# Attended values in a PSUM bank of their own, an MLP ring of three banks, and a re-planned instruction list

## The chip, the cores and the metric

The kernel runs on one core of a Trainium2 chip, as one launch. The metric is the device time of that launch in microseconds (us). Three runs of the kernel before gave 1077.95, 1076.28 and 1081.45 us, so the median is 1077.95 us. One execution was also recorded by the hardware profiler: it took 1077.04 us, and its trace covers a span of 1075.3 us of that.

The core has five engines that work beside each other, each on its own queue in order: PE (matrix products, written to PSUM), DVE (vector engine), ACT (scalar engine), POOL (GpSimd) and SP, which here only starts transfers. An engine waits at an instruction until the semaphores that it names have been raised. PSUM, the memory that PE writes, has eight banks per partition, each of 512 float32; DVE and ACT read it.

## The reference, cut to what matters

```python
# q, k, v: (4, 8, 576, 64); attention with the 32 largest scores of each row
scores = q @ k.T / sqrt(64)
kth    = 32nd largest of each row
attn   = softmax(where(scores >= kth, scores, -1e9))
x      = (attn @ v), heads side by side       # (2304, 512)
# first MLP, 512 -> 2048 -> 512
h = x @ w_in
g = where(h > 0, h, exp(min(h, 0)) - 1)
x = g @ w_out
# second MLP, 512 -> 1024 -> 512
h   = ((x @ w1) * (x @ w2)) @ w3
out = h @ w_out2
```

All inputs are float32 in the reference; the weights reach the kernel as 64-bit words, of which it makes float32 values on the chip, and of these a float16 pair (high and low part) for three float16 products per float32 product.

## The kernel before, in words

**Tiles.** The 2304 tokens are 18 tiles of 128. Nine chunks of two tiles each run through attention and then through the MLP. For a chunk, attention goes over four pairs of heads and the two tiles: 72 steps in all (and eight of them straddle two batches, so that they have two segments).

**One attention step.** SP loads a tile of q (`qr`), ACT and POOL split it (L414, L415). For each of the two heads PE forms 128 x 576 scores as two halves of 288 columns, one in each of the two banks of the PSUM tile `psS` (L435, four matmuls, called QK below), and ACT copies them to `s` (L437, the score copy). DVE finds the 32 largest with four MAX8 (L445) and three MATCH_REPLACE8 (L447). ACT turns the scores to weights (L460, L462), ACT and POOL split them to float16 pairs `pi` (L470, L471), a transposing DMA brings them to `pt` (L473). PE multiplies them by the values (L489, 28 matmuls for a segment, called AV below) into an accumulator `psA`; column 64 of each head is the sum of the weights. ACT copies the sums (L500), DVE inverts them (L503) and multiplies (L506, to `xf`), ACT and POOL split the result (L509, L510), and a small transposing DMA puts it into the MLP's input `x` (L511).

**PSUM before.** `psS` has two banks, `psY` two, and the ring `psR` four, so all eight are taken. The two accumulators `psA` are columns 288 to 417 of the two banks of `psS`, behind the score columns, and are used in turn.

**MLP.** A unit A is 24 matmuls of 256 columns (L748 to L750) into one bank of `psR`; ACT reads it twice (L760 and L769). A unit O (L785 to L787) adds to `psY`. A unit B is 24 matmuls (L827 to L829) into one bank of `psR`, read by ACT (L837, or L846) and DVE (L847). A unit D (L862 to L864) uses a bank of `psR` too. `rot()` hands out the banks of the ring in the order in which the program is written.

**Weights.** Before and beside the first chunks, 72 blocks of weights are loaded and made float32 (`load64`): ACT writes a helper value into a bank of the ring (L540), DVE reads it (L541), ACT and POOL finish (L542, L543). `norm` (L335, L337, L340, L341) measures the size of a set of blocks by way of one or two banks.

**What sets the order.** Nothing runs in the order in which it is written. `Program.op` gathers every operation with its engine, an estimated cost, what it reads and writes, and a due time, to which the table `OFF` adds a number for its group (for example `A2:PE`). `emit` plays the list through a model of the engines and takes, whenever an engine is free, the ready operation with the lowest rank; the model's order is what each engine then gets. For a transfer the model has a time at which it lands (L179). The model orders by the keys that an operation names: in the kernel before `psA` has a key of its own, apart from that of `psS`.

Of the kernel before, what the change touches and what calls it, by code (L numbers as in the profile page):

```python
# [8 lines left out]
F32 = mybir.dt.float32  # L9
# [30 lines left out]
OFF = {":DVE": 12998, "A0:ACT": 1029, "A0:PE": 7709, "A0:POOL": 27517, "A1:ACT": 718, "A1:PE": -1966, "A1:POOL": -5070, "A2:ACT": 9368, "A2:PE":  # L40
# [25 lines left out]
       -37249, "att8x:SP": 2491, "attsa:ACT": -34761, "attsa:PE": -24674, "attsk:ACT": -25447, "attsk:POOL": -12314, "attsk:SP": 6109, "attsm:ACT":  # L66
       58721, "attsm:POOL": 42862, "attsp:ACT": -13632, "attsp:POOL": 6842, "attsp:SP": 1004, "attsq:ACT": -6686, "attsq:POOL": 29332, "attsq:SP":
       2937, "attss:ACT": -4807, "attss:PE": 439, "attst:DVE": 42919, "attsv:ACT": 36078, "attsv:DVE": 24193, "attsv:SP": 27657, "attsx:ACT": 19116,
# [3 lines left out]
       "w_in.c:PE": 6093, "w_in.n:DVE": -7844, "w_in.n:PE": 4153, "w_in:ACT": 4398, "w_in:DVE": -6625, "w_in:POOL": -6043, "w_in:SP": -40971,  # L72
       "w_out.c:ACT": -366, "w_out.c:DVE": -7456, "w_out.c:PE": -21835, "w_out.n:DVE": -33383, "w_out.n:PE": -12498, "w_out:ACT": -1295, "w_out:DVE":
       11860, "w_out:POOL": 17259, "w_out:SP": 13558, "w_v0:DVE": -35479, "w_v0:PE": 32785, "w_v0:SP": -8488, "w_v1:DVE": -18213, "w_v1:PE": 29747,
       "w_v1:SP": 53184, "w_v:DVE": -41841}
# [18 lines left out]
class Program:  # L94
# [30 lines left out]
    def emit(self):  # L125
# [22 lines left out]
        for _ in range(n):  # L148
# [23 lines left out]
            if e == "SP":  # L172

                if len(done) >= 8:
                    t = max(t, done[-8])
                begin = max(dma, t + (1100.0 if lat < 500.0 else 1275.0))
                free[e] = max(t + lat, begin + 131.0) if lat > 1300.0 else t + lat
                dma = begin + cost
                end = dma + 900.0  # L179
                done.append(end)  # L180
            else:
                end = free[e] = t + cost
# [13 lines left out]
def kernel(ctx: ExitStack, tc: tile.TileContext, qd, kd, vd, vn, w_in, w_out, w1, w2, w3t, w4, out,  # L196
# [56 lines left out]
    psAs = [psS[:, i, 288:418].rearrange("p (h d) -> p h d", h=2) for i in range(2)]  # L253
    psY = ring("psY", 2, [128, 2, 256], F32, psum)
    psR = ring("psR", 4, [128, 512], F32, psum)
    psN, pnk = psY[0].rearrange("p a b -> p (a b)")[:, 0:128], ("psY", 0)
    banks = [0, 1]
# [136 lines left out]
    def attention(c, t0, n):  # L394
# [6 lines left out]
        for pair in range(4):  # L401
            base = (t0 * 8 + pair * n * 2 + PAR["a0"] * (c == 0) + PAR["a1"] * (c == 1)) * STEP
            for t in range(n):
# [76 lines left out]
                pa = nxt("psA", 2)  # L480
                psA, pak = psAs[pa], ("psA", pa)
                for bb, c0, c1 in segs:
                    vs = Vc[bb, pair]

                    def av(vs=vs, c0=c0, c1=c1, pt=pt, psA=psA):
                        for hh in range(2):
                            for j in range(14):
                                d = 65 if j < 9 else 64
                                T.matmul(psA[c0:c1, hh, 0:d], lhsT=PT[pt][:, hh, j % 9, c0:c1], rhs=VV[vs][:, j, hh, 0:d], start=j == 0, stop=j == 13, skip_group_check=True)  # L489
                    op("PE", 930, av, [("v", vs), ("vl", vs), ("pt", pt, 0), ("pt", pt, 1)], [pak], p5)  # L490
# [6 lines left out]
                for c0, c1 in ((0, r1), (r1, 128)):  # L497
                    if c0 < c1:
                        sc_, sk_ = (scal(f"rho{vb}")[c0:c1], [("rho", vb)]) if c0 < r1 else (1.0, [])
                        op("ACT", 190, lambda psA=psA, dn=dn, c0=c0, c1=c1, sc_=sc_: A.activation(dn[c0:c1], psA[c0:c1, :, 64], AF.Copy, scale=sc_, bias=1e-9), [pak, *sk_], [K("dn")], p5)  # L500
# [4 lines left out]
                def xfin(xf=xf, dn=dn, psA=psA):  # L505
# [17 lines left out]
    def load64(dst, key, src, shape, pr, slots_, nm, whole=False):  # L523
# [14 lines left out]
        lb = 2 if nm == "w12" else 2 + nxt("low", 2)  # L538
# [48 lines left out]
    def prep_v(b, pr):  # L587
# [12 lines left out]
        norm(pieces, nv, kb, pr)  # L600
# [319 lines left out]
    for c, n in enumerate(chunks):  # L920

        s1 = starts[c] + n
        for b in range(batch(s1) + 1 if c else 1, batch(s1 + (chunks[c + 1] if c + 1 < len(chunks) else 0)) + 1):
            keep, banks[:] = banks[:], [3] if len(banks) < 4 else banks
            prep_v(b, (s1 * 8 + PAR["pvb"]) * STEP)
            banks[:] = keep
        attention(c, starts[c], n)
        if c >= 1:
# [3 lines left out]
            banks[:] = [0, 1] if c == 1 else [0, 1, 2, 3]  # L932
# [58 lines left out]
```

## Time and profile before

| | |
|---|---|
| median of three runs | 1077.95 us |
| profiled execution | 1077.04 us |
| span of its trace | 1075.3 us |
| PE busy | 983.4 us, 91% of the span |
| DVE busy | 889.3 us, 83% |
| ACT busy | 830.3 us, 77% |
| POOL busy | 696.6 us, 65% |
| transfers | 174.97 MB, mean 163 GB/s |

Busy time is that of the instructions of an engine's datapath; waiting at a semaphore is idle time. A wait is named by the line that waited and the line that released it. Matmuls overlap in their pipeline, so PE counts as busy where one is still draining: the step from one matmul to the next is shorter than the time of one. PEclk is the clock that PE was granted as a share of the full one.

### The profile page before, as it was taken

What the parts mean: (1) busy time and instruction counts of PE and PEld (TensorE: products, weight loads), DVE (VectorE), ACT (ScalarE), POOL (GpSimd) and SP (SyncE); (2) the same over time, 40 slices, a digit from 0 to 9 for tenths busy, and PEclk for the clock granted to TensorE, in tenths of its full rate; (3) what the DMA queues carried; (4) which work ended last, traced back from release to release, by engine and by line L of the source; (5) the groups of instructions that cost most, each with busy time, mean ns of one, the idle gap of its engine ahead of it and who ended that gap; (6) DMA issues with size and microseconds to landing.
All of it is one profiled execution on the core that took longest, in us unless ns stands there. A gap on an engine that the chain in (4) does not pass through costs nothing. (4 is left out here: it accounts for less than half of the span.)

```text
span 1075.3 us, 24646 instructions
## 1 busy us (share of the span) xinstructions
PE 983.4 (91%) x9132; PEld 778.6 (72%) x9132; DVE 889.3 (83%) x1968; ACT 830.3 (77%) x1521; POOL 696.6 (65%) x743
## 2 busy tenths in 40 slices
PE   4486899988899989989999999999999999999998
PEld 2333455677787778868887887788778877887875
DVE  4999999999999889998968999998899999810010
ACT  6999887898989867878887797798778878824512
POOL 4967565699478645776884597488547846645611
PEclk9998999989899999999999999999999999999999
DMA  9979997498675794577877738686855373032001
GB/s 362 391 224 297 288 257 173 146 269 178 157 176 164 190 201 116 106 184 182 202 195 180 161 47 198 175 197 156 183 147 118 95 160 69 2 63 63 1 1 40
DMA packets 255384, 174.97 MB, mean 163 GB/s; under 512 B 196640, under 2 KB 223264, under 8 KB 255264
## 3 DMA queue, kind: packets, MB, share of 16 engines
q1 hardware_dynamic: 255264, 173.41, 63.3%
q8 instruction: 71, 1.16, 0.5%
q14 instruction: 49, 0.40, 0.1%
HBM read 104.56 MB, written 21.61 MB: 117 GB/s over the span
## 5 line engine op out<-in xcount | busy, mean ns | idle before, releaser
L445 DVE MAX8 m<-wk 128x8 f32<-128x576 f32 x432 | 311.3, 747 | 0.8
L471 POOL TENSOR_TENSOR pi<-s,pi 128x576 f16<-128x576 f32 x144 | 185.2, 1294 | 92.3 <-ACT pi L470 72.1
L447 DVE MATCH_REPLACE8 wk<-m,wk 128x576 f32<-128x576 f32 x288 | 212.4, 742 | 0.0
L786 PE MATMUL psY<-g,wout 128*128 128x256 f16 x576 | 157.6, 274 | 1.5 <-POOL g L772 1.5
L748 PE MATMUL psR<-x,win 128*128 128x256 f16 x576 | 157.2, 273 | 1.5 <-ACT t L837 0.8
L827 PE MATMUL psR<-x,w 128*128 128x256 f16 x576 | 158.4, 275 | 0.0
L785 PE MATMUL psY<-g,wout 128*128 128x256 f16 x576 | 158.1, 274 | 0.0
L828 PE MATMUL psR<-x,w 128*128 128x256 f16 x576 | 157.9, 274 | 0.0
L829 PE MATMUL psR<-x,w 128*128 128x256 f16 x576 | 157.8, 274 | 0.0
L787 PE MATMUL psY<-g,wout 128*128 128x256 f16 x576 | 157.6, 274 | 0.0
L750 PE MATMUL psR<-x,win 128*128 128x256 f16 x576 | 157.0, 273 | 0.0
L749 PE MATMUL psR<-x,win 128*128 128x256 f16 x576 | 157.0, 273 | 0.0
L435 PE MATMUL psS<-kt,qh 128*128 128x288 f32 x320 | 113.8, 370 | 17.0 <-ACT s L437 11.3
L460 ACT ACTIVATE s<-s,m 128x576 f32<-128x576 f32 x144 | 108.5, 771 | 25.2 <-DVE m L445 25.0
L437 ACT ACTIVATE s<-psS 128x576 f32<-128x576 f32 (+1 forms) x160 | 103.1, 644 | 29.0 <-POOL pi L471 9.6
L445 DVE MAX8 m<-s 128x8 f32<-128x576 f32 x144 | 104.7, 746 | 14.0 <-ACT s L437 14.0
L470 ACT ACTIVATE pi<-s 128x576 f16<-128x576 f32 x144 | 95.8, 677 | 24.0 <-DMA pt<-pi 23.8
L462 ACT ACTIVATE s<-s,ty 128x576 f32<-128x576 f32 x144 | 106.8, 768 | 6.1 <-POOL ty L456 6.0
L447 DVE MATCH_REPLACE8 wk<-m,s 128x576 f32<-128x576 f32 x144 | 106.3, 742 | 0.0
L489 PE MATMUL psS<-vv,pt 128*128 128x65 f16 (+3 forms) x2240 | 83.5, 194 | 23.5 <-ACT s L437 11.8
L489 PEld LDWEIGHTS <-pt 128*128 128x128 f16 (+1 forms) x2240 | 76.6, 101 | 35.1 <-issue 17.8
L770 POOL TENSOR_TENSOR t<-t,t 128x512 f32<-128x512 f32 x72 | 92.3, 1286 | 3.4 <-ACT t L769 2.1
(154 smaller groups left out, 2374.2 us busy)
## 6 DMA issues: line engine op xcount, KB each, us to landing
kt<-kd SPq DMA_DIRECT2D x32, 576.0 KB, 4.5
vv<-vd SPq DMA_DIRECT2D x32, 455.0 KB, 4.6
qr<-qd SPq DMA_DIRECT2D x72, 128.0 KB, 3.2
raw<-kd SPq DMA_DIRECT2D x32, 288.0 KB, 4.4
kd<-kt SPq DMA_DIRECT2D x16, 576.0 KB, 4.0
w<-w_in SPq DMA_DIRECT2D x16, 512.0 KB, 5.9
w<-w_out SPq DMA_DIRECT2D x16, 512.0 KB, 6.7
w<-w3t SPq DMA_DIRECT2D x16, 512.0 KB, 5.7
```

The lines of the kernel that those rows point to most:

```text
L445: op("DVE", 665, lambda r=r, src=src, m8=m8, hh=hh: V.max(m8[:, hh, 8 * r:8 * r + 8], src), [skey], [mk], p1 + PAR["ot"] * STEP)
L447: op("DVE", 727, lambda r=r, src=src, w=w, m8=m8, hh=hh: V.match_replace(w, m8[:, hh, 8 * r:8 * r + 8], src, -3.0e38), [skey, mk], [k], p1 ...
L471: op("POOL", 1240, lambda Y=Y, PIs=PIs, hh=hh: G.tensor_tensor(PIs[:, hh, S:2 * S], Y[:, hh], PIs[:, hh, 0:S], op=OP.subtract), hks, [pk], ...
L489: T.matmul(psA[c0:c1, hh, 0:d], lhsT=PT[pt][:, hh, j % 9, c0:c1], rhs=VV[vs][:, j, hh, 0:d], start=j == 0, stop=j == 13, skip_group_check= ...
L748: T.matmul(o, lhsT=hi(W)[:, cs], rhs=X[:, 0, kd_, 0:N], start=kd_ == 0, stop=False)
L749: T.matmul(o, lhsT=hi(W)[:, cs], rhs=X[:, 1, kd_, 0:N], start=False, stop=False)
L785: T.matmul(o, lhsT=hi(W)[:, cs], rhs=rh, start=ft == 0 and m % 2 == 0, stop=False, skip_group_check=True)
L786: T.matmul(o, lhsT=hi(W)[:, cs], rhs=rl, start=False, stop=False, skip_group_check=True)
L787: T.matmul(o, lhsT=lo(W)[:, cs], rhs=rh, start=False, stop=ft == 15, skip_group_check=True)
L827: T.matmul(o, lhsT=hi(W)[:, cs], rhs=X[:, 0, kd_, 0:N], start=kd_ == 0, stop=False)
L828: T.matmul(o, lhsT=hi(W)[:, cs], rhs=X[:, 1, kd_, 0:N], start=False, stop=False)
L829: T.matmul(o, lhsT=lo(W)[:, cs], rhs=X[:, 0, kd_, 0:N], start=False, stop=kd_ == 3)
```

## The change

The accumulator `psA` gets a PSUM tile of its own, so a bank of its own, and there is one of it where there were two. The ring `psR` has three banks where it had four. Chunk 0's preparation has bank 0 of it alone for `rot()` where it had 0 and 1; from chunk 2 on `rot()` goes over three banks. The helper value of `load64` goes to bank 2 for the weights of both products of the second MLP (`w12`, `w34`), and to banks 1 and 2 in turn for the others; before it was 2 for `w12`, and 2 and 3 in turn for the others, `w34` among them. `prep_v` takes its banks from `psY` as long as the ring has fewer than three. The model's landing time of a transfer becomes 1500 ns (large transposes), 1900 ns (small transposes) or 1100 ns (others) behind its data, where it was 900 ns for all. Every number of the table `OFF` is new.

```diff
-OFF = {":DVE": 12998, "A0:ACT": 1029, "A0:PE": 7709, "A0:POOL": 27517, ...
+OFF = {":DVE": 13807, "A0:ACT": -12479, "A0:PE": 9089, "A0:POOL": 28926, ...
...
-                end = dma + 900.0
+                end = dma + (1500.0 if lat > 1300.0 else 1900.0 if lat > 1000.0 else 1100.0)
...
-    psAs = [psS[:, i, 288:418].rearrange("p (h d) -> p h d", h=2) for i in range(2)]
+    psA = psum.tile([128, 2, 65], F32, name="psA")
     psY = ring("psY", 2, [128, 2, 256], F32, psum)
-    psR = ring("psR", 4, [128, 512], F32, psum)
+    psR = ring("psR", 3, [128, 512], F32, psum)
     psN, pnk = psY[0].rearrange("p a b -> p (a b)")[:, 0:128], ("psY", 0)
-    banks = [0, 1]
+    banks = [0]
...
-                pa = nxt("psA", 2)
-                psA, pak = psAs[pa], ("psA", pa)
+                pak = "psA"
...
-        lb = 2 if nm == "w12" else 2 + nxt("low", 2)
+        lb = 2 if nm in ("w12", "w34") else 1 + nxt("low", 2)
...
-    def prep_v(b, pr):
+    def prep_v(b, pr, kind="rot"):
...
-        norm(pieces, nv, kb, pr)
+        norm(pieces, nv, kb, pr, kind)
...
-            keep, banks[:] = banks[:], [3] if len(banks) < 4 else banks
-            prep_v(b, (s1 * 8 + PAR["pvb"]) * STEP)
-            banks[:] = keep
+            prep_v(b, (s1 * 8 + PAR["pvb"]) * STEP, "y" if len(banks) < 3 else "rot")
...
-            banks[:] = [0, 1] if c == 1 else [0, 1, 2, 3]
+            banks[:] = [0, 1] if c == 1 else [0, 1, 2]
```

On PE, at the AV of the 26th segment (it starts at 384.61 us in the trace of before), the list of the kernel before reads as follows; LDWEIGHTS loads the stationary operand, and the bracket names what an instruction waits for (DMAHW is a transfer, Activation is ACT).

```order
L786 MATMUL psY_152<-g_132,wout 128x256
L787 LDWEIGHTS wout
L787 MATMUL psY_152<-g_132,wout 128x256
L489 LDWEIGHTS pt_122 [waits DMAHW6_49]
L489 MATMUL psS<-vv_114,pt_122 64x65 [waits Activation_49]
```

The same segment in the changed kernel, whose lines here stand one lower (L488 is L489 of before, L786 is L787):

```order
L786 LDWEIGHTS wout
L786 MATMUL psY_153<-g_132,wout 128x256
L435 MATMUL psS<-kt_111,qh_105 128x288 [waits DMAHW4_49,Activation_49]
L435 MATMUL psS<-kt_111,ql_107 128x288 [waits Pool_49]
L435 MATMUL psS<-kt_111,qh_105 128x288
L435 MATMUL psS<-kt_111,ql_107 128x288
L488 LDWEIGHTS pt_122 [waits DMAHW6_49]
L488 MATMUL psA<-vv_114,pt_122 64x65 [waits DVE_49]
```

A QK now stands right ahead of the AV, which waits for the transfer and for DVE, no longer for ACT.

On ACT, in the stage in which the weights of the second MLP are made float32, the list of before has the helper values (L540) in two banks, `psR_155` and `psR_156`:

```order
L540 ACTIVATE psR_155<-w_99 128x512 [waits DMAHW3_49,DVE_49]
L542 ACTIVATE pp<-w_99 128x512
L567 ACTIVATE wout<-w_100,sc 128x512 [waits PE_49,Activation_49]
L542 ACTIVATE pp<-w_99 128x512 [waits DMAHW4_49]
L567 ACTIVATE wout<-w_100,sc 128x512 [waits PE_49,Activation_49]
L540 ACTIVATE psR_155<-w_99 128x512 [waits DVE_49]
L379 ACTIVATE vv_115<-raw,sc 128x8x64 [waits DMAHW6_49]
L567 ACTIVATE wout<-w_100,sc 128x512 [waits PE_49,Activation_49]
L509 ACTIVATE xt_136<-xf_137 128x128
L540 ACTIVATE psR_156<-w_99 128x512 [waits DMAHW7_49]
```

and that of the changed kernel (L539 is L540 of before) in `psR_156` alone:

```order
L539 ACTIVATE psR_156<-w_99 128x512 [waits DVE_49]
L541 ACTIVATE pp<-w_99 128x512 [waits DMAHW3_49]
L566 ACTIVATE wout<-w_100,sc 128x512 [waits PE_49,Activation_49]
L460 ACTIVATE s_116<-s_116,m_145 128x576
L566 ACTIVATE wout<-w_100,sc 128x512 [waits PE_49,Activation_49]
L460 ACTIVATE s_116<-s_116,m_145 128x576
L539 ACTIVATE psR_156<-w_99 128x512 [waits DVE_49]
L566 ACTIVATE wout<-w_100,sc 128x512 [waits PE_49,Activation_49]
L541 ACTIVATE pp<-w_99 128x512 [waits DMAHW5_49]
L462 ACTIVATE s_116<-s_116,ty_149 128x576 [waits Activation_49]
L539 ACTIVATE psR_156<-w_99 128x512 [waits DVE_49]
```

Each helper value there waits for DVE's read of the one before it; in the list of before the third went to the other bank and waits for its transfer only.

## Rows read from the trace of the kernel before

**Rows 1.** Busy time by stretch: us, busy of each engine (instructions), PEclk, DMA share, GB/s.
```profile
0.00:200.00 200.00, 150.29 (x754) 81.92 (x755) 181.52 (x386) 166.63 (x298) 130.36 (x132) 0.97 0.90 271
200.00:400.00 200.00, 181.36 (x1900) 152.75 (x1898) 189.48 (x418) 176.56 (x326) 146.28 (x150) 0.96 0.77 192
400.00:600.00 200.00, 192.69 (x1966) 162.53 (x1963) 183.08 (x415) 158.35 (x298) 137.52 (x153) 1.00 0.71 168
600.00:800.00 200.00, 191.72 (x1993) 161.15 (x1991) 186.69 (x415) 164.81 (x306) 136.48 (x151) 1.00 0.68 158
800.00:916.00 116.00, 112.73 (x1129) 95.21 (x1128) 114.03 (x256) 95.96 (x178) 79.78 (x91) 1.00 0.49 108
916.00:1075.30 159.30, 154.63 (x1403) 125.03 (x1401) 34.49 (x85) 68.00 (x122) 66.23 (x70) 1.00 0.12 28
```

**Rows 2.** Instructions on psS: duration min/median/max, first and last start.
```profile
L435 PE MATMUL psS<-kt,ql x320: 289/294/547, 15.4 to 916.1; 128*128 128x288 f32 x160
```

**Rows 3.** Waits of PE, 200 to 400 us: total, times, longest.
```profile
PE psS L489 <- ACT s L437: 7.0, 6, 2.9
...
PE psS L489 <- DMA pt<-pi: 1.8, 4, 0.5
...
PE psS L489 <- DVE xf L506: 1.0, 1, 1.0
PE psS L435 <- ACT ty L500: 0.9, 1, 0.9
```

**Rows 4.** Waits of PE, 400 to 916 us.
```profile
PE psS L489 <- DMA pt<-pi: 6.3, 10, 1.3
PE psS L489 <- ACT s L437: 3.6, 5, 1.5
...
PE psS L435 <- DVE xf L506: 2.4, 4, 0.8
...
PE psR L748 <- ACT t L837: 0.8, 1, 0.8
PE psS L435 <- ACT ty L500: 0.5, 1, 0.5
```

**Rows 5.** Timeline, 383.5 to 386 us: start, us, instruction, idle before and releaser.
```profile
383.90 0.65 ACT L437 ACTIVATE s<-psS 128x576 f32<-128x576 f32 x1 [0.29 <-POOL pi L471]
...
384.61 1.58 PE L489 MATMUL psS<-vv,pt 128*64 128x65 f16 x42 [2.88 <-ACT s L437]
```

**Rows 6.** Busy time by stretch, around two stretches of lower clock.
```profile
274.00:279.80 5.80, 3.92 (x50) 3.16 (x49) 5.13 (x18) 5.19 (x13) 2.85 (x4) 1.00 1.13 309
279.80:286.60 6.80, 5.88 (x26) 4.34 (x27) 5.80 (x18) 5.42 (x13) 2.44 (x4) 0.50 0.84 156
...
381.00:385.60 4.60, 1.72 (x42) 1.50 (x41) 4.60 (x10) 3.17 (x5) 1.48 (x2) 1.00 1.10 294
385.60:389.00 3.40, 3.40 (x42) 3.15 (x38) 0.93 (x2) 0.26 (x1) 1.08 (x1) 0.50 1.05 251
```

**Rows 7.** DMA issues: count, KB if plain, median us from issue to landing.
```profile
pt<-pi SPq DMA_TRANSPOSE x144, 3.9
```

**Rows 8.** Groups of instructions: busy us, mean ns of one, idle before and releasers.
```profile
L506 DVE TENSOR_TENSOR xf<-psS,ty 128x128 f32<-128x128 f32 x72 | 20.3, 282 | 12.6 <-ACT s L437 5.4 <-PE psS L435 3.8 <-issue 0.9
...
L503 DVE RECIPROCAL ty<-ty 128x2 f32<-128x2 f32 x72 | 10.8, 154 | 23.3 <-ACT ty L500 23.0
...
L500 ACT ACTIVATE ty<-psS 128x2 f32<-128x2 f32 (+1 forms) x64 | 10.2, 167 | 11.6 <-PE psS L489 5.7 <-PE psS L435 4.5 <-DVE xf L506 1.1
```

**Rows 9.** The same view: helper values of the weights, then readers of a B unit.
```profile
L541 DVE SCALAR_TENSOR_TENSOR w<-w,psR 128x512 int32<-128x512 int32 x60 | 40.1, 678 | 4.0 <-ACT psR L540 3.6 <-issue 0.4
L540 ACT ACTIVATE psR<-w 128x512 int32<-128x512 uint32 x60 | 37.6, 636 | 7.0 <-DMA w<-w3t 3.0 <-DMA w<-w_in 2.4 <-DMA w<-w_out 1.5
...
L847 DVE SCALAR_TENSOR_TENSOR t<-psR,sc,t 128x256 f32<-128x256 f32 x54 | 25.3, 474 | 47.5 <-ACT t L846 47.4
L846 ACT ACTIVATE t<-psR,sc 128x256 f32<-128x256 f32 x54 | 24.9, 468 | 20.5 <-PE psR L829 20.2 <-DMA out_dram<-t 0.2
```

More of the change, by code (lines that the diff above doesn't have):

```diff
@@ L38 @@
            pvb=-3829.627, lag1=-475.176, lagb=401.111)
-OFF = {":DVE": 12998, "A0:ACT": 1029, "A0:PE": 7709, "A0:POOL": 27517, "A1:ACT": 718, "A1:PE": -1966, "A1:POOL": -5070, "A2:ACT": 9368, "A2:PE":
[25 rows of a table removed]
-       -37249, "att8x:SP": 2491, "attsa:ACT": -34761, "attsa:PE": -24674, "attsk:ACT": -25447, "attsk:POOL": -12314, "attsk:SP": 6109, "attsm:ACT":
-       58721, "attsm:POOL": 42862, "attsp:ACT": -13632, "attsp:POOL": 6842, "attsp:SP": 1004, "attsq:ACT": -6686, "attsq:POOL": 29332, "attsq:SP":
-       2937, "attss:ACT": -4807, "attss:PE": 439, "attst:DVE": 42919, "attsv:ACT": 36078, "attsv:DVE": 24193, "attsv:SP": 27657, "attsx:ACT": 19116,
[3 rows of a table removed]
[L72 to L75, printed above, removed]
+OFF = {":DVE": 13807, "A0:ACT": -12479, "A0:PE": 9089, "A0:POOL": 28926, "A1:ACT": 1887, "A1:PE": 1481, "A1:POOL": -6842, "A2:ACT": 12564, "A2:PE":
[25 rows of a table added]
+       -31006, "att8x:SP": -7783, "attsa:ACT": -35277, "attsa:PE": -26655, "attsk:ACT": -32653, "attsk:POOL": -8699, "attsk:SP": 1080, "attsm:ACT":
+       65030, "attsm:POOL": 51251, "attsp:ACT": -17693, "attsp:POOL": 9395, "attsp:SP": 6312, "attsq:ACT": -8541, "attsq:POOL": 34851, "attsq:SP":
+       1875, "attss:ACT": -12797, "attss:PE": -8952, "attst:DVE": 49668, "attsv:ACT": 31908, "attsv:DVE": 21919, "attsv:SP": 16024, "attsx:ACT":
[3 rows of a table added]
+       "w_in.c:PE": 10958, "w_in.n:DVE": -1688, "w_in.n:PE": 13297, "w_in:ACT": 7341, "w_in:DVE": -15198, "w_in:POOL": -10845, "w_in:SP": -55636,
+       "w_out.c:ACT": -938, "w_out.c:DVE": -15709, "w_out.c:PE": -21068, "w_out.n:DVE": -35012, "w_out.n:PE": -11456, "w_out:ACT": 4851, "w_out:DVE":
+       21248, "w_out:POOL": 24755, "w_out:SP": 20119, "w_v0:DVE": -51831, "w_v0:PE": 18056, "w_v0:SP": -23242, "w_v1:DVE": -16660, "w_v1:PE": 25930,
+       "w_v1:SP": 54158, "w_v:DVE": -44716}
 def conv_modes(n, d, g):
@@ L479, in attention, with av @@
                 p5 = pr + PAR["oa"] * STEP
-                pa = nxt("psA", 2)
-                psA, pak = psAs[pa], ("psA", pa)
+                pak = "psA"
                 for bb, c0, c1 in segs:
                     vs = Vc[bb, pair]
-                    def av(vs=vs, c0=c0, c1=c1, pt=pt, psA=psA):
+                    def av(vs=vs, c0=c0, c1=c1, pt=pt):
                         for hh in range(2):
@@ L499, in attention, with xfin @@
                         sc_, sk_ = (scal(f"rho{vb}")[c0:c1], [("rho", vb)]) if c0 < r1 else (1.0, [])
-                        op("ACT", 190, lambda psA=psA, dn=dn, c0=c0, c1=c1, sc_=sc_: A.activation(dn[c0:c1], psA[c0:c1, :, 64], AF.Copy, scale=sc_, bias=1e-9), [pak, *sk_], [K("dn")], p5)
+                        op("ACT", 190, lambda dn=dn, c0=c0, c1=c1, sc_=sc_: A.activation(dn[c0:c1], psA[c0:c1, :, 64], AF.Copy, scale=sc_, bias=1e-9), [pak, *sk_], [K("dn")], p5)
                 part("x")
                 op("DVE", 70, lambda dn=dn: V.reciprocal(dn, dn), [K("dn")], [K("ri")], p5)
-                def xfin(xf=xf, dn=dn, psA=psA):
+                def xfin(xf=xf, dn=dn):
                     V.tensor_tensor(xf.rearrange("p (h d) -> p h d", h=2), psA[:, :, 0:64],
```

56 rows, old and new, of the table OFF are left out of this document.

## The prediction

> **What bounds the kernel now.** I read the busy time by stretch first [rows 1]: the reader is to see how much of each stretch PE leaves idle, and what DVE does there. PE is idle for 200 - 150.3 = 49.7 us up to 200 us, 18.6 us from 200 to 400, 7.3, 8.3 and 3.3 us in the three stretches up to 916 us, and 4.7 us behind that. The last QK starts at 916.1 us [rows 2]; what follows is matrix work at 97% of PE, and in the changed instruction order the same PE work stands behind the last QK as before. So the end moves by as much as the last QK moves, and the last QK moves by what PE waits ahead of it. DVE is the second bound: from 400 to 916 us it is busy for 183.1 + 186.7 + 114.0 = 483.8 of 516 us, 94%, where PE has 497.1 us, 96%. Neither can run far ahead of the other, since DVE works on what QK makes.
>
> Then the waits of PE by cause [rows 3, 4]. Three of them come from the bank that scores and accumulators share: AV behind the score copy L437 (7.0 and 3.6 us), QK behind L506 (2.4 us) and L500 (0.9 and 0.5 us), and AV behind L506 (1.0 us). Together 8.9 us from 200 to 400 and 6.5 us from 400 to 916: 15.4 us. AV behind its transposing transfer takes 1.8 and 6.3 us. The timeline shows one case whole [rows 5]: the score copy runs from 383.90 for 0.65 us, and the AV, whose columns it does not touch, starts at 384.61, after 2.88 us of idle PE. In the instruction order of before, 39 QK name DVE among their waits and 26 AV name ACT.
>
> **What the change takes away.** In the new order no QK waits for DVE, and 14 AV wait for ACT (which now reads the accumulator alone, L500). So the 15.4 us can go: that is one end, and nothing is the other, since an instruction that has one wait less may meet the next. With DVE at 94% some of the time saved on PE comes back as a wait for scores or for `pi`; I take two thirds, -10 us.
>
> The Trainium skill, page "PSUM — Partial Sum Buffer", section "PSUM bank collisions raise a hardware error", says that two engines must be kept apart by bank, not by address; the trace agrees, as the 2.88 us show, and by that rule alone the whole 15.4 us would go.
>
> The clock belongs to this too. PE had a granted clock of 0.50, the 1.2 GHz level, from 279.8 to 286.6 and from 385.6 to 389.0 us [rows 6]. Ahead of the first PE was busy for 3.92 of 5.80 us, ahead of the second for 1.72 of 4.60, and the second gap is the wait of rows 5. At the full clock the 5.88 and 3.40 us of PE work would take half: 4.6 us in all at most, 0 at least. I take -2.
>
> **The later landing times.** A large transpose lands 3.9 us after its issue in the median [rows 7]. The model now puts it 0.6 us later than before, so AVs are placed behind more other work. The most that this can take away is the 1.8 + 6.3 = 8.1 us of waiting; the least is a loss, where an AV placed later holds up L506 and through it the MLP's input: I bound it by 3 us, half of the larger wait. I take -2: the transfer stays as long as it is, and DVE's share is as before.
>
> **One accumulator.** In the new order 49 AV rows name DVE as a wait, against 7: an AV must wait until L506 of the step before has read. Behind a waiting AV the next QK and MLP matmuls stand in PE's queue, and DVE waits for that QK. The release takes 167 + 154 + 282 ns of L500, L503 and L506, and if all idle time ahead of them were part of it, 11.6/64 + 23.3/72 + 12.6/72 us more: 0.6 + 0.7 = 1.3 us [rows 8]. Between AVs of different steps the new order has always at least 24 matmuls of 256 columns; at 154.63/1403 = 0.110 us a matmul [rows 1] that is 2.6 us, and in 16 of 71 places it is under 5 us. (Before, six pairs stood with nothing between.) So the chain fits with 1.3 us to spare, and only a queue on DVE or ACT eats that up. Bounds: 0, and 16 times the 1.0 us that the one AV waited for L506 [rows 3], 16 us. I take +1, that row once.
>
> **Three banks for the MLP.** PE now waits little for a bank of the ring: 0.8 us, once, in 516 us [rows 4]. In the new order 122 matmul rows of A and B units carry a wait, against 108. A unit is 24 matmuls, 2.6 us, so three banks leave 5.3 us for the readers of the last but two, where four left 7.9. The readers of a B unit take 468 + 474 ns [rows 9]. Bounds: 0, and 14 more waits of these 0.94 us, 13 us; I take +2, above the row, because PE leaves no room between units in the last 159 us [rows 1].
>
> **The start.** The helper values L540 of w34 have one bank, so the next must wait for DVE's L541: 636 + 678 ns a block, 1.3 us [rows 9]. In the order 56 of 72 name DVE, against 47. ACT's idle time ahead of L540 is 7.0 us now, nearly all for transfers, and other ACT work stands between, as the order shows. Bounds: 0 and 9 x 1.3 = 12 us; I take +1. That the first product sums have one bank costs nothing that I can see, since those blocks arrive one by one.
>
> **Sum.** -10 - 2 - 2 + 1 + 2 + 1 = -10 us, on the profiled execution's 1077.0 us: 1067 us. The median of the runs shown is 0.9 us above that execution, so 1068 us. All instructions stay; the new table also moves hundreds of operations for which no row gives a price, which is why the range is wider than the terms.
>
> **The rivals.**
>
> - *DVE takes over* (1077 us). What PE saves is waited for again as scores: DVE's 94% speaks for it, and from 800 to 916 us it is busy for 114.0 of 116 us. Against it: from 400 to 800 us it leaves 30.2 us idle [rows 1]. Only the 8.9 us ahead of 400 us would count, by half, and the costs of 4 us offset that: 1077.0 - 4.5 + 4 + 0.9 = 1077 us, and 1074 to 1080 about it.
> - *The ring becomes the bound* (1092 us). The readers of a bank sit in the queues of ACT and DVE behind score work of 0.7 us an instruction. There are 72 A and 72 B units; if each waits 0.17 us on average for its bank, that is 24 us, and with the -10 us from the shared bank's waits 14 us are lost: 1077.0 + 14 + 0.9 = 1092 us. It decides from 0.07 us a unit (10 us). For it: the 0.94 us of L846 and L847 start only when ACT comes round, and the 14 extra waits. Against it: 0.8 us of such waiting now, and the model knows that there are three banks. The Trainium skill, page "Perfetto Trace Analysis", section "Matmuls", says that independent matmul groups should rotate through different banks so that the reading of one overlaps the next group; this speaks against both the third bank and the single accumulator. The trace has four banks only, so it does not show what the rule would cost.
> - *All of it goes* (1050 us). 15.4 + 4.6 + 8.1 = 28 us, the whole of the waits, with no cost: 1077.0 - 28 + 0.9. Against it: DVE's 94%.
> - *The change doesn't do what it says.* That AV still waits for score copies: the order has 14 ACT waits left, about half of 26, so the gain would be about 5 us, and with the costs of 4 us the time is 1077 us. Unlikely, since the only reader on ACT is L500.
>
> **How the numbers follow.** The forecast, 1060 to 1074 us, has 0.45; DVE 0.22; the ring, or another of the costs in full, 0.22; all of it 0.09; still sharing 0.02. Within 0.5% means 1072.6 to 1083.3 us, about what a measurement of this kernel can tell from no change. Of the forecast's 0.45 I put 0.42 below 1072.6: with "all of it" that is 0.51 for faster. The other 0.03 with DVE's 0.22 and the 0.02 are 0.27 for the same, and the ring's 0.22 is slower. The range reaches from 1052 (most of "all of it") to 1087 us (beyond half of the ring's price); the likeliest case's own range is 1060 to 1074.
>
> **What would show it.** Right, if in the profile after AV waits for L437 and QK for L506 are gone from PE's waits, PE's idle time between 200 us and the last QK falls from 37.5 us to below 30, and the last QK starts near 906 us. The clock step shows in PEclk around 280 and 386 us. The accumulator's cost is AV behind L506, the ring's is L748 or L827 behind ACT or DVE readers, the start's is ACT's L540 behind L541. The prediction is wrong if the last QK is no earlier (DVE idle ahead of MAX8 grows or PE waits elsewhere), or if PE idles behind 916 us by more than the 4.7 us of now.

## The result and the profile after

The kernel after takes 1063.20 us in the median of 4 runs (1060.59 to 1063.52), the kernel before 1079.04 us in 4 runs beside it: a ratio of 0.9849, with an interval of 0.9819 to 0.9879 (all intervals here are for 95%). That is 15.8 us less; -10 us was forecast. The profiled execution of after took 1063.52 us, over a span of 1061.7 us.

Over the whole span PE is busy as follows, with share of the span and instructions:

```profile
PE 978.0 (92%) x9132; PEld 776.7 (73%) x9132; DVE 888.4 (84%) x1968; ACT 826.1 (78%) x1521; POOL 695.2 (65%) x743
```

Line numbers of after are one lower than before's from L489 on (AV is L488, the sums L499, the product L505, the MLP matmuls L747 and L826).

Busy time by stretch of after, with the columns of [rows 1]:

```profile
0.00:200.00 200.00, 152.00 (x757) 82.54 (x758) 182.18 (x387) 168.35 (x299) 131.07 (x131) 0.89 0.93 281
200.00:400.00 200.00, 182.06 (x1968) 155.43 (x1966) 193.98 (x427) 177.36 (x331) 145.79 (x153) 0.97 0.75 188
400.00:600.00 200.00, 193.94 (x1984) 164.30 (x1983) 188.07 (x428) 162.75 (x306) 140.88 (x156) 1.00 0.70 169
600.00:800.00 200.00, 193.60 (x1990) 162.69 (x1987) 189.69 (x420) 165.06 (x309) 137.30 (x151) 1.00 0.65 157
800.00:900.00 100.00, 98.38 (x1012) 83.51 (x1010) 98.25 (x221) 82.77 (x156) 69.31 (x79) 1.00 0.51 113
900.00:1061.70 161.70, 157.99 (x1435) 128.20 (x1433) 36.27 (x90) 69.84 (x125) 70.89 (x75) 1.00 0.12 28
```

From 200 to 900 us PE is idle for 17.9 + 6.1 + 6.4 + 1.6 = 32.0 us, where before it was idle for 37.5 us from 200 to 916 us [rows 1]. The row of the last QK, to set beside [rows 2]:

```profile
L435 PE MATMUL psS<-kt,ql x320: 289/294/547, 15.5 to 903.6; 128*128 128x288 f32 x160
```

It starts 12.5 us earlier, at 903.6 instead of 916.1 us; behind it stand 1061.7 - 903.6 = 158.1 us, where it was 159.2. So 12.5 of the 13.6 us between the two profiled executions lie ahead of the last QK. PE's waits in after, total us, times and longest, first from 200 to 400 us (to set beside [rows 3]):

```profile
PE psR L747 <- ACT t L768: 4.6, 4, 1.8
PE psS L435 <- ACT s L437: 4.1, 3, 3.3
PE psA L488 <- DMA pt<-pi: 3.1, 2, 2.2
```

and from 400 to 900 us (beside [rows 4]):

```profile
PE psS L435 <- ACT s L437: 5.0, 9, 1.2
PE psA L488 <- DMA pt<-pi: 4.3, 6, 1.5
PE psY L785 <- POOL g L771: 2.0, 2, 1.1
PE psR L747 <- ACT t L768: 1.0, 1, 1.0
PE psR L826 <- DVE t L846: 0.4, 1, 0.4
PE psA L488 <- DVE xf L505: 0.2, 1, 0.2
```

All three waits of the shared bank are gone: no AV behind L437, no QK behind the product or the sums. What is left is QK behind the score copy of the scores before it, whose banks it fills, AV behind its transfer, and MLP matmuls behind readers of the ring. Two of these grew. QK behind the score copy took 1.6 us from 200 to 400 and 2.4 us from 400 to 916 us in before,

```profile
PE psS L435 <- ACT s L437: 1.6, 3, 0.9
...
PE psS L435 <- ACT s L437: 2.4, 5, 0.7
```

and takes 4.1 + 5.0 us now: 5.1 us of the 15.4 come back there. The case that the prediction read whole [rows 5], the AV of the 26th segment, now runs right behind a QK with no wait:

```profile
380.03 0.29 PE L435 MATMUL psS<-kt,ql 128*128 128x288 f32 x1
380.25 1.87 PE L488 MATMUL psA<-vv,pt 128*64 128x65 f16 x56
```

The waits of the whole trace by groups (busy us, mean ns of one, idle before and what ended it):

```profile
L747 PE MATMUL psR<-x,win 128*128 128x256 f16 x576 | 157.2, 273 | 5.9 <-ACT t L768 5.6 <-DVE t L846 0.2
L826 PE MATMUL psR<-x,w 128*128 128x256 f16 x576 | 158.0, 274 | 1.2 <-DVE t L846 0.9
L435 PE MATMUL psS<-kt,qh 128*128 128x288 f32 x320 | 111.7, 363 | 19.5 <-ACT s L437 18.4 <-POOL kt L358 0.7
L488 PE MATMUL psA<-vv,pt 128*128 128x65 f16 (+3 forms) x2240 | 82.6, 194 | 10.1 <-DMA pt<-pi 9.3 <-ACT psR L539 0.3 <-DVE xf L505 0.2
L539 ACT ACTIVATE psR<-w 128x512 int32<-128x512 uint32 x60 | 37.6, 632 | 7.8 <-DMA w<-w3t 4.4 <-DMA w<-w_in 2.2 <-DVE w L540 1.0
```

Stretches of lower clock: one of before that [rows 6] does not show,

```profile
225.20:232.00 6.80, 5.12 (x22) 3.98 (x23) 6.69 (x19) 6.80 (x14) 6.64 (x7) 0.50 1.07 271
```

and those of after:

```profile
26.00:56.70 30.70, 16.05 (x72) 10.71 (x73) 30.70 (x70) 27.47 (x49) 26.87 (x24) 0.50 1.02 397
227.40:230.80 3.40, 3.40 (x18) 2.53 (x17) 2.86 (x11) 3.13 (x8) 3.40 (x3) 0.50 1.06 235
278.60:282.00 3.40, 3.40 (x18) 2.62 (x17) 3.40 (x7) 3.38 (x7) 1.85 (x2) 0.50 0.34 122
374.20:377.60 3.40, 3.40 (x18) 2.64 (x16) 2.85 (x7) 3.04 (x7) 2.29 (x4) 0.50 1.13 306
```

The three dips of before between 200 us and the last QK are still there, the first two half as long (3.4 instead of 6.8 us).

### The profile page after: what moved, and what is told of

Read it like the earlier page. It is cut to its first block, busy times and chain, and to the rows that moved or that the text cites. A ratio compares the mean times of both kernels' runs of the same rounds, so it can differ in the third digit from the quotient of the medians.

```text
span 1061.7 us, 24618 instructions
## 1 busy us (share of the span) xinstructions
PE 978.0 (92%) x9132; PEld 776.7 (73%) x9132; DVE 888.4 (84%) x1968; ACT 826.1 (78%) x1521; POOL 695.2 (65%) x743
## 4 chain that ended last, share of the span: by engine, by line
PE 33%; DVE 26%; ACT 16%; DMA 11%; POOL 6%; issue 6%; SPq 1%; DVEq 0%; ACTq 0%; POOLq 0%
DVE m L445 10%; DVE wk L447 8%; PE psR L826 2%; PE psR L827 2%; PE psR L828 2%; PE psY L784 2%; DMA raw<-kd 2%; PE psY L786 2%; PE psY L785 2%; DMA qr<-qd 2%; DMA pt<-pi 2%; PE psR L747 2%; PE psR L748 2%; PE psR L749 2%; PE psY L686 2%
## 5 line engine op out<-in xcount | busy, mean ns | idle before, releaser
L445 DVE MAX8 m<-wk 128x8 f32<-128x576 f32 x432 | 311.2, 746 | 0.8
L747 PE MATMUL psR<-x,win 128*128 128x256 f16 x576 | 157.2, 273 | 5.9 <-ACT t L768 5.6
L785 PE MATMUL psY<-g,wout 128*128 128x256 f16 x576 | 158.1, 275 | 3.3 <-POOL g L771 3.3
L826 PE MATMUL psR<-x,w 128*128 128x256 f16 x576 | 158.0, 274 | 1.2 <-DVE t L846 0.9
L786 PE MATMUL psY<-g,wout 128*128 128x256 f16 x576 | 158.1, 274 | 0.0
L435 PE MATMUL psS<-kt,qh 128*128 128x288 f32 x320 | 111.7, 363 | 19.5 <-ACT s L437 18.4
L460 ACT ACTIVATE s<-s,m 128x576 f32<-128x576 f32 x144 | 108.6, 770 | 23.4 <-DVE m L445 23.2
L437 ACT ACTIVATE s<-psS 128x576 f32<-128x576 f32 (+1 forms) x160 | 102.9, 643 | 16.4 <-PE psS L435 9.7
L445 DVE MAX8 m<-s 128x8 f32<-128x576 f32 x144 | 104.5, 744 | 10.5 <-ACT s L437 10.3
L470 ACT ACTIVATE pi<-s 128x576 f16<-128x576 f32 x144 | 95.0, 676 | 8.7 <-DMA pt<-pi 8.1
L415 POOL TENSOR_TENSOR ql<-qr,qh 128x256 fp32r<-128x256 f32 x72 | 54.1, 752 | 60.8 <-ACT qh L414 57.0
L435 PE MATMUL psS<-kt,ql 128*128 128x288 f32 x320 | 93.4, 305 | 0.1
```

What stands on the lines that cost most here:

```text
L435: T.matmul(psS[:, half, 0:288], lhsT=L[qs][:, hh], rhs=KT[kk][:, hh, half * 288:half * 288 + 288], start=li == 0, stop=li == 1)
L445: op("DVE", 665, lambda r=r, src=src, m8=m8, hh=hh: V.max(m8[:, hh, 8 * r:8 * r + 8], src), [skey], [mk], p1 + PAR["ot"] * STEP)
L747: T.matmul(o, lhsT=hi(W)[:, cs], rhs=X[:, 0, kd_, 0:N], start=kd_ == 0, stop=False)
L785: T.matmul(o, lhsT=hi(W)[:, cs], rhs=rl, start=False, stop=False, skip_group_check=True)
L786: T.matmul(o, lhsT=lo(W)[:, cs], rhs=rh, start=False, stop=ft == 15, skip_group_check=True)
L826: T.matmul(o, lhsT=hi(W)[:, cs], rhs=X[:, 0, kd_, 0:N], start=kd_ == 0, stop=False)
```

## The experiments

Each run stands beside runs of the kernel before on the same chip, and its ratio is to these. The median of before was 1078.58 us for share, share_four, s_only and off_land, 1078.16 us for s_off, s_land, re_after and re_before, 1078.89 us for s_pt, s_late and re_after2, and 1080.00 us for land. "The table" is `OFF`, the numbers that shift the planner's due times.

**The shared bank by itself (share).** The instruction order of after is kept row for row; only the accumulator lies again in columns 288 to 417 of a scores bank, with the freed bank unused. (It is the first bank alone; the kernel before had two accumulators, one in each bank.)

```diff
-    psA = psum.tile([128, 2, 65], F32, name="psA")
+    psA = psS[:, 0, 288:418].rearrange("p (h d) -> p h d", h=2)
```

> The changed kernel with its instruction order kept to the last row, only the accumulator put back into spare columns of the score bank (the bank that gets free stays unused). If the waits by the shared bank are what the change removed, they come back: AV behind the score copy and QK behind the reads of the accumulator, 8 to 15 us on PE between 200 us and the last QK, and the time is 1071 to 1078 us. If the gain lies in the new list and landing times, the time stays within 3 us of 1063.

It took 1068.38 us (6 runs), a ratio of 0.992 (0.9892 to 0.9949): 5.2 us more than after by the medians, 7.7 us by the ratios, so 5 to 8 us; the intervals of the two ratios together leave 3 to 12 us. The waits that come back between 200 us and the last QK are 7.7 + 2.8 + 1.7 + 0.5 = 12.7 us, as expected; the time lies between the two ranges that were named. And share is itself 10.2 us faster than before by the medians, 8.6 us by the ratio (5.5 to 11.6): the new order alone, with the bank shared, carries as much of the gain as the bank, or more. The groups of QK and AV in share:

```profile
L435 PE MATMUL psS<-kt,qh 128*128 128x288 f32 x320 | 110.2, 359 | 24.3 <-ACT s L437 13.5 <-DVE xf L505 6.6 <-ACT ty L499 2.8
L488 PE MATMUL psS<-vv,pt 128*128 128x65 f16 (+3 forms) x2240 | 82.0, 194 | 12.4 <-ACT s L437 8.4 <-DMA pt<-pi 3.2 <-DVE xf L505 0.5
```

The shared bank's waits come back: 8.4 + 6.6 + 2.8 + 0.5 = 18.3 us. But AV's wait for transfers falls from 9.3 to 3.2 us and QK's behind L437 from 18.4 to 13.5, 11.0 us together, which leaves 7.3: a wait at the shared bank lies partly over a wait that comes next anyway. One step shows it. In share, from the timeline (start us, us, instruction, idle before and its releaser):

```profile
367.32 0.38 PE L435 MATMUL psS<-kt,qh 128*128 128x288 f32 x1
...
369.77 2.28 SPq L473 DMA_TRANSPOSE pt<-pi  x1
...
372.03 0.68 ACT L470 ACTIVATE pi<-s 128x576 f16<-128x576 f32 x1 [3.15 <-DMA pt<-pi]
...
372.93 0.63 ACT L437 ACTIVATE s<-psS 128x576 f32<-128x576 f32 x1
373.61 0.59 PE L488 MATMUL psS<-vv,pt 128*128 128x65 f16 x8 [4.18 <-ACT s L437]
```

and the same step in after:

```profile
368.42 0.38 PE L435 MATMUL psS<-kt,qh 128*128 128x288 f32 x1
...
370.35 0.58 PE L488 MATMUL psA<-vv,pt 128*128 128x65 f16 x14
...
371.03 2.12 SPq L473 DMA_TRANSPOSE pt<-pi  x1
...
373.10 0.60 PE L488 MATMUL psA<-vv,pt 128*128 128x65 f16 x14 [2.17 <-DMA pt<-pi]
```

With the shared bank all 28 matmuls of the AV wait 4.18 us for the score copy, which stands on ACT behind L470, which waits for a transfer. With a bank of its own the first 14 matmuls run in that time, and the other 14 then wait 2.17 us for the second transfer. So PE is idle for 2.17 us here where it was for 4.18: half of the wait at the shared bank had another one under it.

The Trainium skill, page "PSUM — Partial Sum Buffer", section "PSUM bank collisions raise a hardware error", says that engines are to be kept apart by bank, not by address. The run agrees: the columns are disjoint and the waits are back.

**A fourth bank for the MLP (share_four).** As share, but the freed bank becomes a fourth bank of the ring from the second chunk on, in the same instruction order. Its lines are 18 higher.

```diff
...
-    psR = ring("psR", 3, [128, 512], F32, psum)
+    psR = Four(ring("psR", 4, [128, 512], F32, psum))
...
```

`Four` takes each unit's bank from a fixed list.

> As share, and the bank that got free is a fourth one of the MLP ring from chunk 2 on, again with the same instruction order. If three banks cost time, PE's waits at A and B units behind the ring's readers go, and it is 2 to 5 us faster than share. If the planner's order already fits three banks, within 1 us of share.

It took 1070.82 us (6 runs; ratio 0.9933, 0.9911 to 0.9954), not faster than share: 2.4 us slower by the medians, 1.4 by the ratios, which the intervals don't tell from nothing. PE's waits from 200 to 400 us, in share

```profile
PE psR L747 <- ACT t L768: 4.5, 4, 1.8
```

and in share_four:

```profile
PE psR L765 <- ACT t L786: 2.2, 3, 1.6
```

The fourth bank takes 2.3 us of these waits away and gains no time. So three banks cost nothing that these runs can measure, with the accumulator in a scores bank as here.

**Layout and numbers apart.** s_only has after's banks with before's table and landing times:

> The changed PSUM layout alone, planned anew with the old table and the old landing times. If the shared bank is the cause, most of the gain is here: 1063 to 1071 us. If it is the list and the landing times, 1076 us or more; a table tuned for another layout may cost on top of that, up to 1090.

off_land has before's banks with after's table and landing times:

> The old PSUM layout with the new table and the new landing times. If the shared bank is the cause, 1074 to 1084 us, with AV behind the score copy among PE's waits as before. If it is the list and the landing times, 1060 to 1068 us.

s_land has after's banks and landing times with before's table:

> The changed layout and the new landing times with the old table. Against the layout alone with the old table (1095 us) it shows what the landing times do: 1085 us or less if they help by themselves, 1092 to 1100 us if not.

The edits are `OFF = {...}` and line 179, or the banks, taken whole from the other kernel. They took 1094.96 us (ratio 1.0154, 1.0123 to 1.0185), 1095.78 us (1.0169, 1.0141 to 1.0197) and 1092.69 us (1.0139, 1.0092 to 1.0185): all 14 to 17 us slower than before. The first lies above the 1090 us that were named as its end, the second outside both of its ranges, the third in the range for "not". Against the same banks with their own table the wrong one costs more on the new layout, about 30 us (1094.96 and 1092.69 against 1063.20), than on the old one, 17 us (off_land). A table goes with its layout: planned with the other one's table, no part of the change gains anything. (share gains, and it keeps the list itself.) The AV group of s_land:

```profile
L488 PE MATMUL psA<-vv,pt 128*128 128x65 f16 (+3 forms) x2240 | 85.7, 196 | 24.0 <-DMA pt<-pi 13.3 <-DVE xf L505 9.3 <-ACT pp L541 1.1
```

Here the single accumulator does cost waits, 9.3 us behind L505; in after, with its own table, 0.2 us.

**How much a new plan by itself changes (re_after, re_after2, re_before).** One planner number that has nothing to do with the change is nudged, so that PE's order changes in many places: compared place by place with after, 1776 of its 9132 matmuls differ in line in re_after and 3919 in re_after2, 3727 in s_pt below.

```diff
-  cpw=1084.595
+  cpw=1090.0    # re_after; 1130.0 in re_after2, 1079.0 on the kernel before in re_before
```

> The changed kernel planned anew with one number of the ranking nudged by 0.5% (the weight of the remaining path, 1084.6 to 1090.0); everything else as in the changed kernel. It shows how much of the time hangs on the exact order that the table gives. If the layout carries the gain, 1061 to 1069 us. If the table is fitted to one order, 1070 to 1085 us.

> The changed kernel planned anew with the weight of the remaining path at 1130.0 instead of 1084.6, a larger nudge that moves about as many rows of PE as the landing time alone does. If a nudge of this size costs nothing by itself, 1060 to 1067 us; if the table is fitted to its order, 1069 to 1080 us, and then the 11 us of the old landing times prove less.

> The kernel before planned anew with the same number nudged the other way (1084.6 to 1079.0), which moves most of its rows. If the exact order matters little, 1075 to 1084 us; if its table too is fitted to one order, 1085 to 1100 us.

The two of after took 1062.30 us (ratio 0.9859, 0.9818 to 0.99) and 1063.75 us (0.9859, 0.9806 to 0.9912), no different from after. The one of before took 1087.39 us (1.0075, 1.0044 to 1.0105), 8 to 9 us more than before, in the range for a table fitted to one order. So after's gain doesn't hang on one lucky order, as far as two nudges show, while a new order of before can cost 9 us by itself.

**The landing times (s_off, s_pt, s_late, land).** s_off is after with before's landing time for all transfers, s_pt with it for the large transposes alone, s_late with a still later one for these.

```diff
-                end = dma + (1500.0 if lat > 1300.0 else 1900.0 if lat > 1000.0 else 1100.0)
+                end = dma + 900.0                                # s_off
+                end = dma + (900.0 if lat > 1300.0 else ...)     # s_pt
+                end = dma + (2000.0 if lat > 1300.0 else ...)    # s_late
```

> The changed kernel (layout and table) planned with the old landing time of 900 ns. If the landing times carry a part of the gain of their own, AV waits longer for its transfer than in the changed kernel (9 us there), 15 us or more, and the time is 1070 us or more. If they only belong to the table, it is like any other nudge of the plan.

> The changed kernel planned with the old landing time (900 ns) for the large transposes alone, the ones that AV waits for; the other transfers keep the new ones. If it is this landing that the new plan gains by, AV waits for its transfer 14 to 18 us instead of 9 us and the time is 1069 to 1076 us. If any nudge of the plan costs as much, the time is the same but those waits stay near 9 us; if it is the other transfers, 1061 to 1066 us.

> The changed kernel planned with large transposes landing 2000 ns behind their data instead of 1500. If the waits of AV go on falling with the planned landing, they are 6 us or less and the time is 1058 to 1063 us. If 1500 is right and more only puts AV off, or if the table fits the other plan, 1064 to 1075 us.

s_off took 1074.52 us (ratio 0.9971, 0.9946 to 0.9995), s_pt 1074.22 us (0.9948, 0.9924 to 0.9973): 11 us more than after by the medians and 11 to 13 by the ratios, so the large transposes' number alone does it. Both times are in the ranges for a gain by the landing, and AV's wait in s_pt is just above its 14 to 18 us. s_late took 1068.86 us (0.9897, 0.9856 to 0.9938): its waits fell as named, its time did not. The QK and AV groups in s_pt:

```profile
L435 PE MATMUL psS<-kt,qh 128*128 128x288 f32 x320 | 111.6, 363 | 15.3 <-ACT s L437 14.1 <-POOL kt L358 0.7 <-ACT ty L499 0.2
L488 PE MATMUL psA<-vv,pt 128*128 128x65 f16 (+3 forms) x2240 | 85.8, 195 | 19.2 <-DMA pt<-pi 18.5 <-ACT psR L539 0.3 <-DVE xf L505 0.3
```

and the QK and AV groups in s_late:

```profile
L435 PE MATMUL psS<-kt,qh 128*128 128x288 f32 x320 | 112.2, 365 | 25.2 <-ACT s L437 23.2 <-ACT ty L499 0.9 <-POOL kt L358 0.7
L488 PE MATMUL psA<-vv,pt 128*128 128x65 f16 (+3 forms) x2240 | 82.8, 195 | 5.5 <-DMA pt<-pi 5.5
```

AV's wait for its transfer falls from 18.5 through 9.3 to 5.5 us as the number goes from 900 through 1500 to 2000, but QK waits longer behind L437 each time: 14.1, 18.4 and 23.2 us. The two together are 32.6, 27.7 and 28.7 us, and of the three numbers the middle one is best in time too. The two waits give 4.9 us between s_pt and after, though, where the times differ by 11: less than half of it is seen in these rows.

land is the kernel before with after's landing times and nothing else.

```diff
-                end = dma + 900.0
+                end = dma + (1500.0 if lat > 1300.0 else 1900.0 if lat > 1000.0 else 1100.0)
```

> The kernel before (old layout, old table) planned with the new landing times alone. If later landing times help any plan by themselves, AV's waits for its transfer fall from 10 us to 6 us or less and the time is 1068 to 1075 us. If a table belongs to the layout and the landing times it was made with, 1083 to 1096 us, whatever those waits do.

It took 1079.07 us (ratio 0.9983, 0.9958 to 1.0008): no difference, and in neither of the two ranges. Its groups of the first MLP matmul, QK and AV:

```profile
L748 PE MATMUL psR<-x,win 128*128 128x256 f16 x576 | 158.7, 275 | 5.5 <-DMA x<-xt 3.9 <-ACT t L837 1.1 <-ACT t L769 0.4
L435 PE MATMUL psS<-kt,qh 128*128 128x288 f32 x320 | 112.3, 365 | 20.4 <-ACT s L437 10.7 <-ACT ty L500 5.1 <-DVE xf L506 3.4
L489 PE MATMUL psS<-vv,pt 128*128 128x65 f16 (+3 forms) x2240 | 81.0, 194 | 14.9 <-ACT s L437 8.5 <-DMA pt<-pi 2.8 <-DVE xf L506 1.6
```

AV waits only 2.8 us for transfers, but 3.9 us come up as the MLP waiting for its input, QK behind the readers of the accumulator takes 5.1 + 3.4 us, and 8.5 us of AV's waits still go to the score copies. With the old banks and table the later landing buys nothing.

## Why the prediction was right in direction and short in size

- *Shared-bank waits, -10 us forecast.* The mechanism is as said: the 15.4 us are gone from PE's waits. The size came out smaller: with the order held fixed the bank is worth 5 to 8 us, a third to a half of its waits and not two thirds, though the intervals (3 to 12 us) don't exclude 10. I put the rest down to DVE; in share it is the transfers and score copies that lie under the same waits.
- *All the other terms, 0 us forecast (-2 - 2 + 1 + 2 + 1).* Here the sum fell short. share has everything of the change but the bank, and is 8.6 us faster than before. The sum gave the new list no price of its own ("hundreds of operations for which no row gives a price"); it is worth as much as the bank, or more.
- *Landing times, -2 us forecast: the term that was mis-sized, as far as the runs show.* Taken back from after, with its table kept, they cost 11 us (s_pt, s_off). The step that does not hold is "the most that this can take away is the 1.8 + 6.3 = 8.1 us of waiting". That bound read the transfer waits of before, where a part of them was covered by AV's wait at the shared bank: in the same order they are 3.2 us with the bank shared (share) and 9.3 with it apart (after), and 18.5 with the old landing time besides (s_pt). The two terms lean on each other: 5 to 8 and 11 are each measured with the other in place and are not to be added up, and land shows that without the bank and the table the second is nothing. That the landing number is worth 11 us in itself is not shown: the waits give 4.9 of them, and a new plan alone cost before 8 to 9 us (re_before).
- *Clock, -2 us forecast.* About that, but not in the way I said: the dips did not go, and a third one, which I left out, got shorter as well. PE's work at the lower level between 200 us and the last QK was 5.12 + 5.88 + 3.40 us and is three times 3.40 us now; half of the difference, as in the forecast, is an estimate of 2.1 us. Ahead of the last dip PE is still idle: 2.17 us, for a transfer and at another AV than in before.
- *Single accumulator, +1.* 0.2 us in after. The price exists, 9.3 us of waits in s_land, but only with a table made for two accumulators.
- *Ring of three, +2.* PE's waits for it (L747 and L826) come to 7.1 us, 4.6 of them between 200 and 400 us on L768, a reader of the A units, not where I looked for them (the B units at the end). In time it is nothing that share_four can measure. (Before, PE waited for the ring for 1.1 us from 400 to 916 us, not 0.8: the view behind [rows 4] has 0.3 us more behind L760.)
- *Start, +1.* ACT's L539 waits 1.0 us behind L540, as said. No cost is seen: by 200 us PE has come as far as before (757 matmuls against 754).
- *Signs named.* The last QK was to start near 906 us and starts at 903.6. PE's idle time from 200 us on was to fall below 30 us and is 32.0: this sign failed. The idle time falls by 5.5 us from 200 us on and by 1.7 us ahead of that (49.7 to 48.0), which is not all of the 12.5 us; PE's busy time falls too, from 983.4 to 978.0 us. Most of that is waiting as well: a stop begins while the matmuls before it still drain, and so long PE counts as busy. Counted from one matmul's start to the next, over the 7731 matmuls ahead of the last QK (the same work in both), the steps that are over 0.25 us longer than the usual one of their kind exceed it by 106 us in before and by 95 us in after: about 11 of the 12.5 us.
- *Rivals.* That DVE takes over is not seen: from 400 to 900 us it is busy for 188.07 + 189.69 + 98.25 = 476.0 of 500 us, 95%, against 94%, but that is the same work in less time, and the wait of its first MAX8 (L445) for the score copy falls from 14.0 to 10.3 us. The ring as the bound is refuted by the time itself and by share_four. That all 28 us go was too much, since 9.3 us of transfer waits remain. That AV still waits for score copies is refuted by the waits above.

What stays open: which of the table's numbers carry it, and how much of the 11 us belongs to the landing number in itself and how much to a table that was made with it. The landing edits re-plan the whole list, and only two nudges say that a re-plan of after is harmless as such. No run has a table made anew for the old banks either, so how much of the new order's 8.6 us the old layout could have had with a better table is not known.

## What to carry to other kernels

A wait that ends at a shared bank may lie over another wait that would have followed: hold the instruction order fixed and put the sharing alone back, and price it by that and not by its rows (18.3 us of waits were 5 to 8 us of time here). The same run prices what else was changed: the new order alone was worth 8.6 us, as much as the bank or more. Two terms of a sum that end at the same instruction must be priced together, for taking the one away lays the other bare (AV's transfer waits, 3.2 us with the bank shared and 9.3 us with it apart, in one order). Numbers tuned for the other layout cost 17 us on the old layout and about 30 us on the new, so a layout is judged only with numbers made for it, and a nudge of an idle number tells how much a new plan moves the time by itself.

## What was not expected of the hardware

From 26.0 to 56.7 us the granted clock of PE is 0.50, the 1.2 GHz level, in after's profiled execution, 30.7 us on end; in before's it is 1.00 there. Yet the QK matmuls of the two take the same time up to 50 us, first in before, then in after:

```profile
L435 PE MATMUL psS<-kt,ql x6: 442/442/502, 38.1 to 48.5; 128*128 128x288 f32 x6
L435 PE MATMUL psS<-kt,ql x6: 442/442/502, 38.1 to 48.5; 128*128 128x288 f32 x6
```

From 57 to 87 us, at 1.00 in both, the median is 293 and 292 ns. So a granted clock of 1.00 in the record was no sign of full speed there, and the long stretch at 0.50 cost nothing up to 50 us. In the time of whole executions none can be seen either: after took 1063.52 us at a mean granted clock of 0.974 and 1063.46 us at 0.991.
